# Weight tiles of a fused attention and feed-forward kernel: writes moved to ACT's queue, loads one stage earlier, whole tiles, one more resident

## The chip, the cores and the metric

The kernel runs on one core of a Trainium2 chip. The metric is the device time of one execution in microseconds (us). Engines: PE (TensorE, matrix products), DVE (VectorE), ACT (ScalarE), POOL (GpSimd), and SP (SyncE), which issues DMAs. PE's clock has two levels, 1.2 and 2.4 GHz; the profile gives the granted share of the higher one.

## What is computed

All inputs are float64 on the host; the reference in short:

```python
q_s = softmax(q, axis=-1); k_s = softmax(k, axis=2)      # [8 batches, 8 heads, 576, 64]
attn = q_s @ (k_s^T @ v)                                  # linear attention
x = attn as [4608 tokens, 512]
x = relu(x @ w_in) ** 2 @ w_out                           # 512 -> 2048 -> 512
xn = x / sqrt(mean(x * x) + 1e-6) * rms_g
out = (silu(xn @ w_gate) * (xn @ w_val)) @ w_out2         # 512 -> 1536 -> 512, float32 out
```

## The kernel before

Tokens go in nine blocks j of 512. The first feed-forward stage runs over 9 x 16 units (j, c), one for each chunk c of 128 hidden columns: `p1_A` (L526) multiplies the block by a tile of w_in into `ps_h`, applies ReLU and the square on ACT and splits the result into two float32r halves (`split`, L72: the rounded half on ACT, the rest on DVE); `p1_B` (L538), two units later, multiplies it by a tile of w_out into four accumulators. Each product is three passes over the halves (`mm3`, L92). The second stage (`p2_A`, L654, and `p2_B`, L725) does the same with gate, value and second output weights, the gate and value products by a scheme of seven half-size products (L637).

A weight tile is [128, 2, 512] float32r: 512 KB, two halves. The weights come as float64, and the core converts each tile once, in jobs that run beside the units. `tick` (L308) runs one stage of four successive jobs in this order: `d_split` of job n-3 (rounded half on ACT, L246; the rest on POOL, L247), `d_float` of n-2 (three DVE steps: L230, L238, L242), `d_words` of n-1 (POOL makes s, L211; ACT makes n, L219), `d_load` of n (the raw words by DMA from SP, L192, into one of two `raw` buffers). Behind the rounding, `d_split` writes a tile to device memory (`wd`, L253, SP) unless it is resident. The jobs of the first stage, 32 tiles, are due in the first sixteen units; those of the second stage follow over the next hundred units, where sums of converted tiles (`d_quad`, L267) are made on POOL and split and written one per unit (`d_out`, L259, with two `so` buffers, also from SP).

Eight tiles of the first stage stay resident (`NTAG`, `res1`, L126). The others pass through a ring of seven tiles `ws`; `feed` (L159) loads the next from `wd` when one is used up. In the second stage sixteen are resident (`res2`, L127).

Beside the units runs the attention of the next block for four pairs of heads (`A_STEPS`, L760): load k, q and v from SP (L334, L361), maxima, exponentials and sums on DVE and ACT, transposes and products on PE. For the first block it runs ahead of the first unit, with five ticks strewn in (the letters w in L800).

The library orders each engine's instructions ahead of time with a planner that has its own costs, starting from the order in which they are written; on the chip each queue then runs strictly in that order, and a DMA that waits holds up those behind it on the same queue. How many ticks are due by unit i:

```python
if i < FF1:                                                      # L755
    return min(NJ1 + 2, 3 + sum(d <= i for d in due.values()))
return min(NJ1 + 3 + max(0, i - FF1 - 1) * 2 // 5, len(jobs) + 3)
```

Of the kernel before, what the change touches and what calls it, by code (L numbers as in the profile page):

```python
# [8 lines left out]
F32 = mybir.dt.float32  # L9
F32R = mybir.dt.float32r  # L10
# [14 lines left out]
def attention_moe_kernel(  # L25
# [6 lines left out]
    w_out: bass.AP,  # L32
    w_gate: bass.AP,
    w_val: bass.AP,
    w_out2: bass.AP,
# [11 lines left out]
    NP = H // 2  # L47
    FF1 = w_in.shape[1] // P
    FF2 = w_gate.shape[1] // P
    SF = S // P  # L50
# [50 lines left out]
    NQ = FF2 // 2  # L101
    NTAG = 8
    NX = 8
# [79 lines left out]


    raws, words, floats = {}, {}, {}

    def halves(n, c, r):
        rows = slice(r * (DM // 2), (r + 1) * (DM // 2))
        cols = slice((2 * n + c) * P, (2 * n + c + 1) * P)
        return [w[rows, cols].rearrange("(k p) f -> p k f", p=P) for w in (w_gate, w_val)]  # L190

    def d_load(key):  # L192
        n, c = key
        r = pools["d"].tile([P, 512], U64, tag="raw", name="raw", bufs=2)
        if n == "i":
            src = w_in[:, c * P : (c + 1) * P].rearrange("(k p) f -> p k f", p=P)
            nc.sync.dma_start(out=r.rearrange("p (k f) -> p k f", k=KD), in_=src)
        elif n in ("o", "u"):
            w = w_out if n == "o" else w_out2
            nc.sync.dma_start(out=r, in_=w[c * P : (c + 1) * P, :])  # L200
        else:
            for g, src in enumerate(halves(c, int(n[0]) - 1, int(n[1]) - 1)):
                rv = r.rearrange("p (g k f) -> p g k f", g=2, k=2)
                nc.sync.dma_start(out=rv[:, g], in_=src)
        raws[key] = r
# [102 lines left out]
    def tick():  # L308
        n = ticks[0]
        for stage, ahead in ((d_split, 0), (d_float, 1), (d_words, 2), (d_load, 3)):  # L310
            if 0 <= n - 3 + ahead < len(jobs):
                key = jobs[n - 3 + ahead]
                if key is None:
                    continue
                if stage == d_split and n - 3 + ahead >= NJ1:
                    stage = d_quad
                stage(key)
        ticks[0] += 1

    def wl(key, c):  # L320
# [456 lines left out]
    with ExitStack() as ctx_a:  # L777
# [35 lines left out]
        for i, (j, c) in enumerate(units):  # L813
            if i == FF1:
                ctx_s.close()
                pools["q"] = ctx_q.enter_context(
                    tc.tile_pool(name="qp", bufs=1, reuse_waits="tile")
                )
            p1_A(j, c)
            pending.append((j, c, None))  # L820
            if len(pending) > LAG:
                p1_B(*pending.pop(0)[:2])
            while ticks[0] < n_ticks(i):
                tick()
            if i > FF1 and outs:
                outs.pop(0)()
            for n, ja, hp, f in todo.get(i, ()):
                f(ja, hp)
            if i == n1 - FF1 - 1:
                assert not outs and ticks[0] == len(jobs) + 3  # L830
# [30 lines left out]

_INS = [
    "q",
    "k",
    "v",
    "moe_w_in",
    "moe_w_out",
    "moe2_w_gate",
    "moe2_w_val",
    "moe2_w_out",  # L870
    "moe2_rms_g",
]
_OUTS = [((4608, 512), "float32")]


# [27 lines left out]
```

## Time and profile before

| | us |
|---|---|
| three runs, lowest, median, highest | 1822.58, 1823.58, 1827.39 |
| the profiled execution | 1824.28 |
| its span | 1822.5 |
| PE busy | 1750.0 (96%) |
| PE weight loads busy | 1516.4 (83%) |
| DVE busy | 1163.1 (64%) |
| ACT busy | 744.9 (41%) |
| POOL busy | 227.3 (12%) |

The span runs from the first instruction to the last; the 1.78 us around it belong to the execution. PE's busy time says where it had work, and not how fast. The shares are means over stages with different limits: the attention of the first block fills about the first 34 us, the first stage with conversions the time to some 600 us, the rest of the first stage that to 957 us, and the second stage the remainder.

### The profile page before, as it was taken

The numbers are of one execution on the slowest core, as the hardware profiler recorded it, in microseconds if no ns is written. First come the engines' busy times: TensorE is split into PE (matmuls) and PEld (weight loads), VectorE is DVE, ScalarE is ACT, GpSimd is POOL, SyncE is SP. The second block draws the span as 40 slices with busy tenths as digits, with TensorE's granted clock in tenths as the row PEclk, the third lists the DMA queues.
The fourth block names the chain that finished last, engine by engine and source line by source line (L and its number), as shares of the span: only waits on it lengthen the run. The fifth ranks groups of instructions, "written<-read, shape, count | busy, mean of one in ns | idle before, by whom it ended". The sixth has DMA issues, their size and how long they took to land.

```text
span 1822.5 us, 27487 instructions
## 1 busy us (share of the span) xinstructions
PE 1750.0 (96%) x10298; PEld 1516.4 (83%) x10298; DVE 1163.1 (64%) x2080; ACT 744.9 (41%) x1279; POOL 227.3 (12%) x265
## 2 busy tenths in 40 slices
PE   5888989999999999999999999999999999999998
PEld 3666878778877888888888989898999999999997
DVE  8987987768687654321336666675767676757544
ACT  3654545555545434333443333423233333333322
POOL 4553224333414100000000000000000000000000
PEclk9998999999999999999999999999999999999999
DMA  6778878898878855445767666767676767676673
GB/s 191 228 235 267 269 249 290 268 298 268 299 259 286 267 177 172 160 140 208 256 214 233 221 246 215 242 222 255 209 257 213 255 209 261 212 244 217 214 237 131
DMA packets 190244, 423.35 MB, mean 232 GB/s; under 512 B 57888, under 2 KB 95776, under 8 KB 188960
## 3 DMA queue, kind: packets, MB, share of 16 engines
q1 hardware_dynamic: 190112, 421.60, 69.6%
q8 instruction: 82, 1.34, 0.3%
q14 instruction: 50, 0.41, 0.1%
HBM read 361.76 MB, written 59.77 MB: 231 GB/s over the span
## 4 chain that ended last, share of the span: by engine, by line
PE 76%; DVE 10%; DMA 6%; issue 2%; ACT 2%; SPq 2%; POOL 1%; DVEq 0%; POOLq 0%; ACTq 0%
PE acc L94 31%; PE ps_h L94 15%; PE ps_x L668 8%; PE ps_y L668 8%; PE ps_v L668 8%; PE ps_w L668 4%; DMA kt<-in_k_dram 2%; DMA out_dram<-e 2%; DVE t L242 1%; DVE t L238 1%; PE ps_x L94 1%; DVE g L74 1%; DVE t L230 1%; PE ps_kv L480 1%; DVE mk L381 1%
## 5 line engine op out<-in xcount | busy, mean ns | idle before, releaser
L94 PE MATMUL ps_h<-x,ws 128*128 128x512 f32 x1296 | 328.3, 402 | 5.7 <-POOL ws L247 4.7
L94 PE MATMUL acc<-g,ws 128*128 128x512 f32 x1296 | 315.5, 392 | 7.8 <-ACT ws L246 3.4
L74 DVE TENSOR_TENSOR g<-r,g 128x512 fp32r<-128x512 f32 x252 | 186.9, 742 | 172.6 <-ACT g L73 169.9
L94 PEld LDWEIGHTS acc<-g,ws 128*128 128x128 f32 x1296 | 243.3, 188 | 62.2 <-ACT ws L246 4.2
L94 PEld LDWEIGHTS ps_h<-x,ws 128*128 128x128 f32 x1296 | 242.8, 192 | 59.2 <-POOL ws L247 7.0
L94 PE MATMUL acc<-ws,g 128*128 128x512 f32 x1080 | 267.1, 392 | 0.0
L94 PEld LDWEIGHTS acc<-ws,g 128*128 128x128 f32 x1080 | 195.5, 189 | 36.4
L73 ACT ACTIVATE g<-r 128x512 fp32r<-128x512 f32 x252 | 157.9, 627 | 35.1 <-DVE r L652 30.8
L650 ACT ACTIVATE sg<-c 128x256 f32<-128x256 f32 x108 | 56.5, 523 | 262.8 <-DVE c L683 213.3
L532 ACT ACTIVATE r<-ps_h 128x512 f32<-128x512 f32 x144 | 85.3, 593 | 190.6 <-PE ps_h L94 190.0
L683 DVE TENSOR_TENSOR u<-ps_y,p 128x512 f32<-128x512 f32 x108 | 73.9, 684 | 124.2 <-PE ps_y L668 124.2
L668 PE MATMUL ps_x<-x,ws 128*128 128x256 f32 x972 | 130.5, 284 | 10.1 <-ACT p L699 10.1
L668 PEld LDWEIGHTS ps_x<-x,ws 128*128 128x128 f32 x972 | 122.1, 191 | 11.8 <-ACT p L699 11.7
L668 PEld LDWEIGHTS ps_v<-x,ws 128*128 128x128 f32 x864 | 114.1, 191 | 6.4
L668 PE MATMUL ps_v<-x,ws 128*128 128x256 f32 x864 | 116.0, 282 | 0.0
L94 PE MATMUL ps_h<-x,w 128*128 128x512 f32 x432 | 109.2, 399 | 2.5 <-DVE x L74 1.9
L94 PE MATMUL acc<-g,w 128*128 128x512 f32 x432 | 105.7, 393 | 3.9 <-DVE g L74 1.9
L706 ACT ACTIVATE p<-ps_v 128x512 f32<-128x512 f32 x54 | 32.3, 599 | 174.8 <-PE ps_v L668 174.8
L683 DVE TENSOR_TENSOR c<-ps_v,u 128x512 f32<-128x512 f32 x54 | 37.4, 692 | 100.0 <-PE ps_v L668 99.7
L668 PE MATMUL ps_y<-x,ws 128*128 128x256 f32 x756 | 100.9, 283 | 0.0
L94 PEld LDWEIGHTS acc<-g,w 128*128 128x128 f32 x432 | 81.4, 189 | 21.9 <-DVE g L74 2.3
L94 PEld LDWEIGHTS ps_h<-x,w 128*128 128x128 f32 x432 | 80.6, 190 | 21.8 <-DVE x L74 2.5
(118 smaller groups left out, 2521.0 us busy)
## 6 DMA issues: line engine op xcount, KB each, us to landing
ws<-wd_s SPq DMA_DIRECT2D x135, 512.0 KB, 4.3
ws<-wd_a SPq DMA_DIRECT2D x117, 512.0 KB, 4.5
ws<-wd_i SPq DMA_DIRECT2D x96, 512.0 KB, 4.6
ws<-wd_o SPq DMA_DIRECT2D x96, 512.0 KB, 4.5
ws<-wd_u SPq DMA_DIRECT2D x90, 512.0 KB, 4.1
raw<-in_moe_w_out_dram SPq DMA_DIRECT2D x28, 512.0 KB, 5.3
wd_s<-so SPq DMA_DIRECT2D x24, 512.0 KB, 5.8
x2d<-e SPq DMA_DIRECT2D x36, 256.0 KB, 3.2
```

Of the source, the lines that this page charges most:

```text
L73: nc.scalar.activation(out=dst[:, 0], in_=src, func=AF.Copy)
L74: nc.vector.tensor_tensor(out=dst[:, 1], in0=src, in1=dst[:, 0].bitcast(F32), op=ALU.subtract)
L94: nc.tensor.matmul(ps, lhsT(a), rhs(b), start=first and n == 0, stop=last and n == 2)
L230: nc.vector.tensor_scalar(out=t, in0=sb, scalar1=3, scalar2=0x7FFFFFFF, op0=ALU.logical_shift_left, op1=ALU.bitwise_and,)
L238: nc.vector.scalar_tensor_tensor(out=t, in0=sb, scalar=0x80000000, in1=t, op0=ALU.bitwise_and, op1=ALU.bitwise_or)
L242: nc.vector.tensor_tensor(out=ti, in0=ti, in1=n, op=ALU.add)
L381: nc.vector.tensor_reduce(out=mk, in_=kts[j, hp].rearrange("p h c d -> p h d c"), axis=AX.X, op=ALU.max)
L532: nc.scalar.activation(out=r, in_=ps, func=AF.Relu)
L650: nc.scalar.activation(out=r, in_=h[:, :, 0], func=AF.Sigmoid)
L668: nc.tensor.matmul(ps[:, g * HF : (g + 1) * HF], w[:, wa, (2 * g + kk) * P : (2 * g + kk + 1) * P], x[:, xa, kk, :], start=first and g == ...
L683: nc.vector.tensor_tensor(out=sv(name), in0=in0, in1=in1, op=ALU.add)
L706: nc.scalar.activation(out=sv("p5"), in_=ps, func=AF.Copy)
```

## The change

- Writes of split tiles go from SP to ACT's queue and later in the program: `send` notes the tile, `flush` issues those that are old enough (two ticks for tiles of the first stage, about two units for those of the second). `keep_in_program_order` keeps such a DMA behind the ACT instructions written before it.
- Loads run one tick further ahead (four stages of lead in place of three), with three `raw` buffers in place of two. `n_ticks` gives one tick more by each unit.
- The host lays the weights out in whole tiles: a raw load is one DMA of 128 rows of 4 KB. Before, a w_in tile came in pieces of 1 KB, and a tile of gate and value weights in two DMAs.
- `NTAG` 9 in place of 8: one more resident tile in the first stage, one more in the second.
- Buffers: three `so` in place of two; the gate's `sg` moves to a pool that exists in the second stage alone; the software DMA scratch space is made smaller.

The attention is untouched. The core of the diff:

```diff
-    NTAG = 8
+    NTAG = 9
...
-        r = pools["d"].tile([P, 512], U64, tag="raw", name="raw", bufs=2)
...
+        r = pools["d"].tile([P, 512], U64, tag="raw", name="raw", bufs=3)
+        if n in ("i", "o", "u"):
+            src = {"i": w_in, "o": w_out, "u": w_out2}[n][c]
         else:
...
+            src = w_gv[int(n[1]) - 1, int(n[0]) - 1, c]
+        nc.sync.dma_start(out=r, in_=src)
...
+    late = []
+
+    def send(key, t, after):
+        late.append([after, key, t])
+
+    def flush(all=False):
+        for x in late:
+            x[0] -= 1
+        while late and (late[0][0] < 0 or all):
+            _, key, t = late.pop(0)
+            tc.keep_in_program_order(nc.scalar.dma_start(out=wd[key], in_=flat(t)))
+
     def d_split(key):
         t = slot_tile(key) if key in res1 else ring_tile()
         w_split(t, floats.pop(key), nc.gpsimd)
         if key not in res1:
-            nc.sync.dma_start(out=wd[key], in_=flat(t))
+            send(key, t, 2)
...
-            t = pools["q"].tile([P, 2, 512], F32R, tag="so", name="so", bufs=2)
+            t = pools["q"].tile([P, 2, 512], F32R, tag="so", name="so", bufs=3)
             w_split(t, f(), nc.gpsimd)
-            nc.sync.dma_start(out=wd[key], in_=flat(t))
+            send(key, t, 1)
...
-        for stage, ahead in ((d_split, 0), (d_float, 1), (d_words, 2), (d_load, 3)):
-            if 0 <= n - 3 + ahead < len(jobs):
-                key = jobs[n - 3 + ahead]
+        for stage, ahead in ((d_split, 0), (d_float, 1), (d_words, 2), (d_load, 4)):
+            if 0 <= n - 4 + ahead < len(jobs):
+                key = jobs[n - 4 + ahead]
...
         ticks[0] += 1
+        if n < NJ1 + 4:
+            flush()
...
-        r = gp.tile([P, n, HF], F32, tag="sg", name="sg", bufs=2)
+        r = pools["x"].tile([P, n, HF], F32, tag="sg", name="sg", bufs=2)
...
-            return min(NJ1 + 2, 3 + sum(d <= i for d in due.values()))
-        return min(NJ1 + 3 + max(0, i - FF1 - 1) * 2 // 5, len(jobs) + 3)
+            return min(NJ1 + 3, 4 + sum(d <= i for d in due.values()))
+        return min(NJ1 + 4 + max(0, i - FF1 - 1) * 2 // 5, len(jobs) + 4)
...
             if i > FF1 and outs:
                 outs.pop(0)()
+            if ticks[0] > NJ1 + 4:
+                flush()
...
+                flush(all=True)
...
+    nc = _bacc.Bacc(
+        "TRN2", target_bir_lowering=False, num_devices=1, dynamic_dma_scratch_size=1024
+    )
```

## Rows read from the trace of the kernel before

**Rows 1.** Windows by block: stretch, length, busy PE, PEld, DVE, ACT, POOL; clock, DMA.
```profile
33.70:169.30 135.60, 114.60 (x519) 84.90 (x518) 113.78 (x194) 73.11 (x126) 65.97 (x67) 0.94 0.73 238
169.30:273.00 103.70, 98.94 (x506) 80.81 (x505) 94.02 (x196) 51.67 (x87) 22.84 (x29) 0.98 0.82 258
273.00:372.00 99.00, 97.47 (x505) 79.47 (x504) 74.24 (x143) 50.52 (x85) 35.56 (x36) 1.00 0.86 284
372.00:471.70 99.70, 97.34 (x507) 79.00 (x506) 76.83 (x150) 53.73 (x91) 33.07 (x35) 1.00 0.88 290
471.70:577.00 105.30, 99.97 (x506) 80.88 (x505) 73.65 (x137) 50.19 (x85) 34.62 (x38) 0.98 0.80 272
577.00:676.00 99.00, 97.10 (x505) 79.59 (x504) 68.38 (x135) 48.80 (x81) 17.78 (x21) 1.00 0.73 240
676.00:773.40 97.40, 97.40 (x507) 79.95 (x506) 38.71 (x86) 40.09 (x65) 0.43 (x3) 1.00 0.50 161
```

**Rows 2.** One window of all that follows the conversions.
```profile
638.00:1822.00 1184.00, 1168.29 (x7380) 1053.95 (x7378) 660.11 (x1135) 420.31 (x732) 1.06 (x7) 1.00 0.64 216
```

**Rows 3.** Windows of the first block in two parts.
```profile
33.70:101.00 67.30, 59.32 (x286) 45.09 (x285) 65.09 (x118) 38.70 (x67) 33.87 (x33) 0.97 0.70 226
101.00:169.30 68.30, 55.28 (x235) 39.82 (x234) 48.69 (x77) 34.41 (x59) 32.10 (x34) 0.90 0.75 249
```

**Rows 4.** Groups of POOL, 101 to 169.3 us: busy, mean ns | idle before, releaser.
```profile
L247 POOL TENSOR_TENSOR ws<-t,ws 128x512 fp32r<-128x512 f32 x12 | 15.8, 1322 | 17.6 <-ACT ws L246 17.6
L211 POOL TENSOR_SCALAR s<-raw 128x512 f32<-128x512 f32 x15 | 12.5, 837 | 8.8 <-DMA raw<-in_moe_w_out_dram 5.7 <-DMA raw<-in_moe_w_in_dram 3.0
L247 POOL TENSOR_TENSOR w<-t,w 128x512 fp32r<-128x512 f32 x3 | 3.9, 1295 | 8.9 <-ACT w L246 8.9
```

**Rows 5.** Timeline, 98 to 104 us: start, duration, instruction, [idle before, releaser].
```profile
98.87 0.65 POOL L211 TENSOR_SCALAR s<-raw 128x512 f32<-128x512 f32 x1
...
99.56 0.43 DVE L230 TENSOR_SCALAR t<-s 128x512 uint32<-128x512 uint32 x1
...
100.84 0.69 DVE L242 CUSTOM_DVE_ANT_0 t<-t,n 128x1024 uint16<-128x1024 uint16 x1
...
101.63 0.63 ACT L246 ACTIVATE ws<-t 128x512 fp32r<-128x512 f32 x1 [2.39 <-DVE t L242]
...
102.34 1.28 POOL L247 TENSOR_TENSOR ws<-t,ws 128x512 fp32r<-128x512 f32 x1 [2.82 <-ACT ws L246]
...
103.59 0.65 POOL L211 TENSOR_SCALAR s<-raw 128x512 f32<-128x512 f32 x1
```

**Rows 6.** Waits of SP, 0 to 600 us: total us, times, longest.
```profile
SPq L253 <- POOL ws L247: 68.7, 21, 5.6
...
SPq L350 <- DVE qn L455: 40.3, 9, 7.8
SPq L263 <- POOL so L247: 37.4, 16, 6.0
```

**Rows 7.** DMA issues on the page: count, KB each, median us to landing.
```profile
raw<-in_moe_w_out_dram SPq DMA_DIRECT2D x28, 512.0 KB, 5.3
...
raw<-in_moe_w_in_dram SPq DMA_DIRECT2D x16, 512.0 KB, 4.6
```

**Rows 8.** Groups of DVE, 101 to 169.3 us.
```profile
L242 DVE CUSTOM_DVE_ANT_0 t<-t,n 128x1024 uint16<-128x1024 uint16 x15 | 12.0, 802 | 1.2
L238 DVE SCALAR_TENSOR_TENSOR t<-s,t 128x512 uint32<-128x512 uint32 x14 | 11.6, 827 | 0.3
```

**Rows 9.** Groups of DVE, 33.7 to 101 us.
```profile
L238 DVE SCALAR_TENSOR_TENSOR t<-s,t 128x512 uint32<-128x512 uint32 x15 | 15.8, 1051 | 0.1
L242 DVE CUSTOM_DVE_ANT_0 t<-t,n 128x1024 uint16<-128x1024 uint16 x16 | 15.4, 965 | 0.2
```

**Rows 10.** A group of DVE, 0 to 700 us: the attention's maxima.
```profile
L381 DVE TENSOR_REDUCE mk<-kt 128x128 f32<-128x640 f32 x31 | 40.4, 1303 | 35.7 <-DMA kt<-in_k_dram 29.2 <-POOL kvd L793 4.7 <-POOL kt L338 1.5
```

**Rows 11.** Line 253: issues of a write from SP, ns min/median/max.
```profile
L253 SPq DMA_DIRECT2D wd_i<-ws x12: 320/334/506, 38.9 to 162.7; - x12
```

More of the change, by code (lines that the diff above doesn't have):

```diff
@@ L32, in attention_moe_kernel @@
     w_out: bass.AP,
-    w_gate: bass.AP,
-    w_val: bass.AP,
+    w_gv: bass.AP,
     w_out2: bass.AP,
@@ L47, in attention_moe_kernel @@
     NP = H // 2
-    FF1 = w_in.shape[1] // P
-    FF2 = w_gate.shape[1] // P
+    FF1 = w_in.shape[0]
+    FF2 = w_out2.shape[0]
     SF = S // P
@@ L309, in tick @@
         n = ticks[0]
-        for stage, ahead in ((d_split, 0), (d_float, 1), (d_words, 2), (d_load, 3)):
-            if 0 <= n - 3 + ahead < len(jobs):
-                key = jobs[n - 3 + ahead]
+        for stage, ahead in ((d_split, 0), (d_float, 1), (d_words, 2), (d_load, 4)):
+            if 0 <= n - 4 + ahead < len(jobs):
+                key = jobs[n - 4 + ahead]
                 if key is None:
                     continue
-                if stage == d_split and n - 3 + ahead >= NJ1:
+                if stage == d_split and n - 4 + ahead >= NJ1:
                     stage = d_quad
@@ L829, in attention_moe_kernel @@
             if i == n1 - FF1 - 1:
-                assert not outs and ticks[0] == len(jobs) + 3
+                assert not outs and ticks[0] == len(jobs) + 4
+                flush(all=True)
                 ctx_q.close()
@@ L859, in attention_moe_kernel @@
             p2_B(*u)
[L862 to L873, printed above, removed]
 def kernel(**inputs):
@@ L881 @@
     from concourse.bass_utils import run_bass_kernel_spmd as _run
-    nc = _bacc.Bacc("TRN2", target_bir_lowering=False, num_devices=1)
-    arrays, args = {}, []
-    for name in _INS:
-        a = _np.ascontiguousarray(inputs[name])
-        if a.dtype == _np.float64:
-            a = a.view(_np.uint64)
-        arrays[f"in_{name}_dram"] = a
-        args.append(
-            nc.dram_tensor(
-                f"in_{name}_dram", a.shape, _mybir.dt.from_np(a.dtype), kind="ExternalInput"
-            ).ap()
-        )
@@ L895, with tiles @@
-    for i, (shape, dtype) in enumerate(_OUTS):
-        dt = _mybir.dt.from_np(_np.dtype(dtype))
-        args.append(nc.dram_tensor(f"out_{i}_dram", shape, dt, kind="ExternalOutput").ap())
+    P = 128
+    def tiles(name, dims, order, shape):
+        t = _np.ascontiguousarray(inputs[name]).view(_np.uint64).reshape(dims).transpose(order)
+        return _np.ascontiguousarray(t).reshape(shape)
+    a = {name: _np.ascontiguousarray(inputs[name]) for name in ("q", "k", "v")}
+    d, ff = inputs["moe_w_in"].shape
@@ new lines @@
+    a["w_in"] = tiles("moe_w_in", (d // P, P, ff // P, P), (2, 1, 0, 3), (ff // P, P, d))
+    a["w_out"] = tiles("moe_w_out", (ff // P, P, d), (0, 1, 2), (ff // P, P, d))
+    d, ff = inputs["moe2_w_gate"].shape
+    dims = (2, d // P // 2, P, ff // P // 2, 2, P)
+    t = [
+        tiles(name, dims, (0, 4, 3, 2, 1, 5), (2, 2, ff // P // 2, P, d // 2))
+        for name in ("moe2_w_gate", "moe2_w_val")
+    ]
+    a["w_gv"] = _np.concatenate(t, axis=-1)
+    a["w_out2"] = tiles("moe2_w_out", (ff // P, P, d), (0, 1, 2), (ff // P, P, d))
@@ new lines @@
+    a["rms_g"] = inputs["moe2_rms_g"]
+    nc = _bacc.Bacc(
+        "TRN2", target_bir_lowering=False, num_devices=1, dynamic_dma_scratch_size=1024
+    )
+    arrays, args = {}, []
+    for name in a:
+        arrays[f"in_{name}"] = _np.ascontiguousarray(a[name])
+        dt = _mybir.dt.from_np(arrays[f"in_{name}"].dtype)
+        shape = arrays[f"in_{name}"].shape
+        args.append(nc.dram_tensor(f"in_{name}", shape, dt, kind="ExternalInput").ap())
+    b, h, s, e = a["q"].shape
+    out = nc.dram_tensor("out", (b * s, h * e), _mybir.dt.float32, kind="ExternalOutput")
@@ L898 @@
     with _tile.TileContext(nc) as tc:
-        attention_moe_kernel(tc, *args)
-    r = _run(nc, [arrays], core_ids=[0])
-    got = tuple(r.results[0][f"out_{i}_dram"] for i in range(len(_OUTS)))
-    return got[0]
+        attention_moe_kernel(tc, *args, out.ap())
+    return _run(nc, [arrays], core_ids=[0]).results[0]["out"]
```

13 lines of the change are left out of this document (removed).

## The prediction

> **What bounds the kernel now.** I read the page first: TensorE (PE) is busy 96% of the span (it stands in the table of the page), so a change can gain only what PE loses in some stage. Then the windows, cut at every sixteenth unit of the first feed-forward stage (a unit is one chunk c of one block j; I call a row of sixteen units a block). The seventh window [rows 1] is a block with nothing in its way: 97.4 us, PE busy throughout at full clock. The six before it do the same matmuls beside weight conversion and attention, and take 135.6, 103.7, 99.0, 99.7, 105.3 and 99.0 us: 38.2, 6.3, 1.6, 2.3, 7.9 and 1.6 us more, 57.9 us together. Behind 638 us PE is busy 1168.3 of 1184.0 us [rows 2] and POOL does nothing: no conversion runs there. So the change can act on those 57.9 us, and mostly on the first block.
>
> The first block, cut in two [rows 3], has two limits. Up to 101 us VectorE (DVE) is busy 65.09 of 67.30 us, 97%: it is the bound there. From 101 to 169.3 us DVE is down to 48.69 of 68.30 us, POOL to 32.10, ACT to 34.41, PE to 55.28 at a clock of 0.90: no engine is full, so the stretch is held by a chain. The POOL rows [rows 4] say of what kind: fifteen tiles are split (12 in ring buffers and 3 residents), and before the splits POOL stood idle 17.6 + 8.9 us for ACT's half of the split, and before the first conversion step 8.8 us for the raw DMA. The timeline [rows 5] shows one round: POOL makes s at 98.87, DVE starts on it at 99.56 and ends L242 at 101.53, ACT rounds at 101.63, POOL subtracts at 102.34, and only then, at 103.59, POOL makes the next s. That is 4.7 us for a tile, and 68.3 us by fifteen tiles is 4.55: the stages written to overlap run one tile after another. PE wants two tiles a unit, that is one in 97.4/32 = 3.04 us.
>
> **The change part by part**, against the profiled execution, 1824.28 us (1822.5 of span and 1.78 around it; the median is 0.70 lower).
>
> *Loads one tick further ahead, three raw buffers, writes off SP.* Before, the load of job n stands on SP behind the write of job n-3, which waits for POOL's subtraction. SP waited 68.7 us in 21 such writes, 3.3 us each, and 37.4 us in 16 writes of the second kind [rows 6]. After it, SP holds no write of a weight tile; a load waits for the raw buffer alone, freed two stages before it, and its data has two ticks to come instead of one. The median raw load lands 4.6 us (w_in) or 5.3 us (w_out) after its issue [rows 7], which is more than one tick of 4.55 and less than two. So the raw wait goes, and POOL can make the s of a later tile before it subtracts an earlier one: the loop of [rows 5] opens. What is late next is DVE. Its work in the second stretch is 48.69 us; packed as densely as in the first stretch its instructions get longer, because there POOL runs beside it more: L238 from 827 to 1051 ns and L242 from 802 to 965 ns [rows 8, 9]. That is 14 x 0.224 + 15 x 0.163 = 5.6 us, so 54.3 us, and at 97% filling 56.0 us. 68.3 - 56.0 = 12.3: I take 12 us gained. The bounds: nothing, if the loop stays; and 68.3 less PE's own need, 15 tiles x 3.04 = 45.6, which is 22.7 us. I take the DVE end since the stretch just before it is held by DVE.
>
> In the first stretch DVE is full, so I take zero. One tick more ahead of the first unit moves one tile's three DVE steps behind the attention of block 0; that can cost at most their 0.43 + 0.69 + 0.69 = 1.8 us (durations with POOL idle [rows 5]; L238 taken as L242), and DVE's whole idle time there is 2.2 us, so the bounds are +1.8 and -2.2.
>
> *The same in blocks 2 to 6*, 19.7 us over. kmax of the attention (L381) kept DVE waiting 29.2 us for the k tiles in the first 700 us [rows 10], and those loads stand on SP in order behind the writes. SP's waits there: 37.4 us for the split tiles, which goes, and 40.3 us for the previous q tile (L350 on DVE's qn) [rows 6], which stays as the attention stays. So about half of SP's blocking goes, but a wait on SP only counts where attention ends last, and the attention buffers hold the next loads back anyway. I take a third of 19.7, 6 us, with 0 and 19.7 as bounds. The single loads for the gate and value tiles (24 DMAs fewer to issue, 0.33 us each on SP [rows 11]) lie within this term.
>
> *What is added: 77 writes on ACT's queue* (23 in the first block, 54 of the second stage). No DMA was issued from ACT, so its price is open: the nearest row is SP's, 334 ns for the median write [rows 11], and for 77 of them 25.7 us of ACT over about 570 us. The cover is ACT's idle time, 33.9 of 68.3 us in the second stretch [rows 3]. Behind a write stand ACT's roundings, exponentials and ReLUs. A write leaves two ticks after its split, some 9 us later, where POOL's subtraction takes 1.3 us, so I count no wait with it. Bounds: zero, and all 25.7 us if the cover is gone; I take zero, because ACT idled before the split in waiting for DVE. Three split buffers in place of two carry the later writes.
>
> *Whole tiles in memory.* w_out was read in whole 4 KB rows before and landed in 5.3 us; w_in was read in 1 KB pieces and landed in 4.6 us [rows 7]. Short pieces don't show as slower, so zero; between the two, 0.7 us on 16 loads, 11 us either way if they all stood in the loop, and they leave it by the extra tick.
>
> *One more resident, the gate's buffer moved.* One ring tile less in the first block, 8 loads less in the later blocks and 9 in the second stage, at places where PE waits for no weight; 15.7 us of idle time in 1184 [rows 2] is the whole that could be touched, by less than 2 us either way. Zero.
>
> The sum: 0 - 12 - 6 + 0 = -18, so 1824.28 - 18 = 1806.
>
> **The rivals.**
> *PE becomes the bound* of the second stretch, and the attention loads run freely: -22.7 there and two thirds of 19.7, -13, give 1788.6. For it: DVE had 19.6 us idle in that stretch. Against: DVE is full just before.
> *The loop stays.* The order on each engine's queue is fixed ahead by a planner with its own idea of times. If it still puts the subtraction before the next s, only part of the 8.8 us of raw waits goes, say 3 us, and the 6 us of the later blocks: 1815. For it: the code of before also meant to overlap. Against: its loads came too late for that.
> *POOL takes it back from DVE.* When the loop opens, POOL's 30 steps run while DVE works. If each holds a DVE step back for half its length, that is 15 x 0.66 + 15 x 0.42 = 16.2 us; already paid are 15 x 0.11 for L242 (802 against 690 ns with POOL idle [rows 5, 8]) and 14 x 0.14 for L238, 3.6. So 48.7 + 12.6 = 61.3, at 97% 63.2: 5 us gained in place of 12, and with the 6 us 1813. The Trainium skill (SBUF — State Buffer, "Terms") says that DVE and GpSimd share a pair of ports under a lock held for the full instruction, and that the loser blocks; the trace agrees as far as L242 goes from 690 to 965 ns where POOL is busier.
> *Slower: ACT is held by the writes.* ACT runs in order, and a write that is not ready stops the roundings and ReLUs behind it. On SP a write waited 3.3 us. It decides from 18/77 = 0.23 us a write on PE's path. At 0.4 us each, 31 us: 1824.3 - 18 + 31 = 1837. For it: the DMA's price on ACT is unknown. Against: the two ticks of delay and ACT's idle half.
>
> **How the numbers follow.** Forecast 0.48 (1800 to 1813), PE bound 0.13, loop stays 0.17, POOL takes it back 0.13, slower 0.09. A measurement here tells 0.3% (5.5 us) from no change, so faster means under 1818. Faster: 0.46 of the forecast, 0.13, 0.11 of 0.17, 0.11 of 0.13: 0.81. Same: the rest of these, 0.02 + 0.06 + 0.02, and 0.01 of the last: 0.11. Slower: 0.08. The range goes down to the PE-bound case, 1789, and up past the two small gains to 1822, with their second term at nothing.
>
> **What would show it.** After: a first block of about 123 us; in its second half two s steps of POOL or more between the end of DVE's L242 and the subtraction of that tile, DVE over 90% busy, and POOL's idle time before the splits under 15 us (26.5 before); no wait of SP for POOL; kmax waiting for k under 20 us; DMA rows of ACT of about 0.33 us with no wait for POOL; the stretch of the second stage as long as before within 2 us. A first block over 130 us, or ACT waiting at its writes, makes the forecast wrong; gains behind 700 us would mean that I missed a cause.

## The result, and the profile after

The changed kernel takes 1837.01 us at the median of four runs (1835.74 to 1839.59), the kernel before 1825.19 beside it (1822.58 to 1827.39): a ratio of 1.0067, 95% interval 1.0048 to 1.0086. It is slower by 12 us where 18 us less were forecast. The profiled execution took 1837.18 us, 1835.4 of them span.

Windows of the kernel after at the same units as [rows 1] (stretch, length, busy PE, PEld, DVE, ACT, POOL, clock, DMA share, GB/s):

```profile
33.80:169.20 135.40, 110.56 (x520) 80.27 (x519) 120.62 (x210) 69.35 (x125) 73.60 (x69) 0.96 0.75 253
169.20:277.60 108.40, 99.88 (x505) 81.20 (x504) 89.71 (x189) 54.18 (x91) 30.28 (x34) 0.97 0.76 238
277.60:385.60 108.00, 100.38 (x506) 81.55 (x505) 68.19 (x137) 48.30 (x81) 24.85 (x27) 0.97 0.70 227
385.60:488.60 103.00, 98.74 (x505) 80.48 (x504) 64.88 (x137) 47.45 (x81) 24.59 (x27) 0.98 0.72 237
488.60:593.80 105.20, 100.17 (x505) 81.65 (x504) 67.90 (x137) 48.34 (x81) 24.96 (x27) 0.97 0.73 233
593.80:695.30 101.50, 99.10 (x506) 81.00 (x505) 66.79 (x137) 49.05 (x82) 27.33 (x28) 0.98 0.71 229
695.30:792.60 97.30, 97.30 (x506) 79.89 (x505) 44.50 (x92) 45.70 (x76) 15.52 (x15) 1.00 0.65 217
```

Against [rows 1], the first block is as long as before (135.4), the five behind it take 526.1 us in place of 506.8, the seventh is the same. The rest is the tail, from the start of the last first-stage unit to the end: 868.8 us in place of 875.1. So +19.3 in units 16 to 95, -6.3 in the tail, nothing in units 0 to 15. POOL shows another difference: it still splits in the seventh block (15.52 us busy, 0.43 before), so the conversion is spread over more units.

What PE and ACT wait for from 165 to 700 us (us in total, times, longest), in the kernel before:

```profile
PE ps_x L94 <- DVE kvd L493: 7.8, 5, 4.7
...
ACT so L246 <- DMA wd_s<-so: 21.4, 15, 3.6
...
ACT so L246 <- DMA wd_a<-so: 14.5, 12, 4.0
...
ACT so L246 <- DMA wd_u<-so: 13.8, 8, 2.6
```

and in the kernel after:

```profile
PE ps_x L93 <- DVE kvd L497: 22.7, 7, 6.3
...
ACT so L236 <- DMA wd_s<-so: 33.6, 15, 5.4
...
ACT so L236 <- DMA wd_a<-so: 24.7, 11, 4.5
...
ACT so L236 <- DMA wd_u<-so: 11.5, 5, 4.5
...
ACT r L536 <- POOL so L237: 7.1, 2, 4.2
```

PE waits longer for `kvd`, the k-v matrix that the last product of the next block's attention needs (two lines of the kernel make it, 25.0 us in place of 11.5 with both), and ACT's roundings of the second-stage tiles wait for a free `so` buffer, 69.8 us in place of 49.7. The last line is a ReLU that stood behind a write which waited for POOL's split. The longest wait of PE, 6.27 us at 226.00, shows how the two belong together. ACT in the timeline (start, duration, instruction, [idle before, releaser]):

```profile
209.04 0.33 ACTq L249 DMA_DIRECT2D wd_a<-so  x1
209.42 0.60 ACT L536 ACTIVATE r<-ps_h 128x512 f32<-128x512 f32 x1 [4.17 <-POOL so L237]
...
215.33 0.63 ACT L236 ACTIVATE so<-s 128x512 fp32r<-128x512 f32 x1 [3.99 <-DMA wd_a<-so]
215.39 0.36 ACTq L249 DMA_DIRECT2D wd_s<-so  x1
...
216.42 0.58 ACT L72 ACTIVATE qT<-ps_q 128x512 fp32r<-128x512 f32 x1
...
220.54 0.63 ACT L236 ACTIVATE so<-s 128x512 fp32r<-128x512 f32 x1 [1.72 <-DMA wd_s<-so]
...
221.64 0.72 ACT L435 ACTIVATE ke<-kt 128x640 f32<-128x640 f32 x1
...
292.73 0.33 ACTq L249 DMA_DIRECT2D wd_a<-so  x1
...
296.86 0.63 ACT L236 ACTIVATE so<-t 128x512 fp32r<-128x512 f32 x1 [1.67 <-DMA wd_a<-so]
```

and DVE:

```profile
217.03 0.69 DVE L73 TENSOR_TENSOR qT<-ps_q,qT 128x512 fp32r<-128x512 f32 x1 [3.27 <-ACT qT L72]
...
224.58 0.27 DVE L497 TENSOR_SCALAR kvd<-ps_kv,rk 64x64 fp32r<-64x64 f32 x1
```

A write goes out at 209.04; the rounding behind it waits 3.99 us for its landing; behind that stand the query's rounding (216.42) and, behind the next such wait, the exponential of k (221.64). DVE idles 3.27 us, makes `kvd` from 224.58 on, and PE goes on at 226.00. In the six waits of PE for `kvd` over 1.5 us, ACT had stood at a landing or at POOL's split in the 18 us before. The last two ACT rows show why buffers were short: behind the write at 215.39 the next one goes out at 292.73, so the three tiles rounded last, up to 220.54, kept all three `so` buffers for some 70 us, and the next rounding (296.86) waited for that write's landing. This recurs: on the mean of the 54 writes the issue comes 27.3 us after the end of POOL's split.

### The profile page after: what moved, and what is told of

The parts are those of the page before. It is cut to its first block, busy times and chain, and to the rows that moved or that the text cites. A ratio compares the mean times of both kernels' runs of the same rounds, so it can differ in the third digit from the quotient of the medians.

```text
span 1835.4 us, 27344 instructions
## 1 busy us (share of the span) xinstructions
PE 1754.6 (96%) x10298; PEld 1518.2 (83%) x10298; DVE 1144.0 (62%) x2080; ACT 740.2 (40%) x1279; POOL 239.3 (13%) x265
## 4 chain that ended last, share of the span: by engine, by line
PE 81%; DVE 5%; DMA 3%; ACT 1%; issue 1%; POOL 0%; SPq 0%; DVEq 0%; POOLq 0%; ACTq 0%
PE acc L93 33%; PE ps_h L93 17%; PE ps_x L672 8%; PE ps_v L672 8%; PE ps_y L672 8%; PE ps_w L672 4%; PE ps_x L93 1%; DVE t L228 1%; DMA wd_a<-so 1%; PE ps_kv L484 1%; DVE t L232 1%; DMA wd_s<-so 1%; PE ps_q L471 1%; DVE t L220 1%; DVE g L73 0%
## 5 line engine op out<-in xcount | busy, mean ns | idle before, releaser
L73 DVE TENSOR_TENSOR g<-r,g 128x512 fp32r<-128x512 f32 x252 | 181.5, 721 | 207.2 <-ACT g L72 204.5
L93 PE MATMUL ps_h<-x,ws 128*128 128x512 f32 x1188 | 304.1, 405 | 5.1 <-POOL ws L237 4.9
L93 PEld LDWEIGHTS ps_h<-x,ws 128*128 128x128 f32 x1188 | 225.5, 194 | 55.2 <-POOL ws L237 7.5
L93 PE MATMUL acc<-ws,g 128*128 128x512 f32 x972 | 243.2, 393 | 2.3 <-ACT g L72 2.3
L93 PEld LDWEIGHTS acc<-ws,g 128*128 128x128 f32 x972 | 175.2, 189 | 35.9 <-ACT g L72 3.7
L93 PE MATMUL ps_h<-x,w 128*128 128x512 f32 x540 | 135.0, 397 | 1.4 <-POOL w L237 1.2
L93 PEld LDWEIGHTS ps_h<-x,w 128*128 128x128 f32 x540 | 99.8, 189 | 23.1 <-POOL w L237 1.6
L93 PEld LDWEIGHTS acc<-g,w 128*128 128x128 f32 x432 | 80.8, 188 | 19.3 <-DVE g L73 2.6
```

The lines of the kernel that those rows point to most:

```text
L73: nc.vector.tensor_tensor(out=dst[:, 1], in0=src, in1=dst[:, 0].bitcast(F32), op=ALU.subtract)
L93: nc.tensor.matmul(ps, lhsT(a), rhs(b), start=first and n == 0, stop=last and n == 2)
```

## Experiments

Times are medians beside runs of the kernel before on the same chip; the lengths of stretches come from one profiled execution each. The changed kernel issues 23 first-stage and 54 second-stage writes; expectations below count 13 and 64, which is wrong, and nothing hangs on it. Versions of the kernel before that need more buffers also have the smaller DMA scratch space. Most runs vary one part of the change, in the kernel after or alone in the kernel before. Where "writes" are named, the second-stage ones alone are varied; the run without the pin and the one with all writes from SP take in the first-stage ones.

**The pin alone**, in the kernel after:

```diff
-            tc.keep_in_program_order(nc.scalar.dma_start(out=wd[key], in_=flat(t)))
+            nc.scalar.dma_start(out=wd[key], in_=flat(t))
```

> The changed kernel with the second-stage and first-stage writes still issued late through ACT's queue, but no longer pinned to the program order: the planner may put each write where it likes among ACT's instructions. Theory P (pin): the planner runs the second-stage roundings some 100 us ahead of program order while a pinned write stays behind a gate rounding traced before it, so that two of the three so buffers are held and each rounding on ACT waits for the landing of the write before it. Unpinned writes come right behind their splits; ACT's waits at L236 for wd writes (53 us in 0 to 600 now) fall to under 20, the single PE waits of 1.8 to 6.3 us for kvd in units 16 to 95 go, unit 143 starts at 947 to 953 us instead of 966.6, and the time is 1816 to 1823. Rival Q (ACT's queue itself): a DMA write that waits for its POOL split stands in ACT's queue whatever its place, and holds the roundings behind it; the writes come earlier and so wait longer: time 1833 or more. Rival L (the load lead and the third raw buffer set the planner's order): no change, 1835 to 1839.

Measured: 1846.08 us, ratio 1.0125 (1.0106 to 1.0143). My first theory fell: ACT's waits for landings are all but gone (6.5 us from 165 to 700), and it is slower still. Q's time came, but not by its mechanism alone: units 16 to 47 take 241.3 us (202.8 before) with DVE 88% busy, and units 64 to 95 take 193.4 us, no longer than two blocks with nothing in their way (97.3 each). The conversion has run ahead.

**The writes from SP at the split**, as before, the rest as changed:

```diff
-            send(key, t, 1)
+            nc.sync.dma_start(out=wd[key], in_=flat(t))
```

> The changed kernel with its second-stage writes alone put back where they were: issued by SP right at the split, not late and not on ACT; the 13 or so first-stage writes stay late on ACT, and the raw buffers, the layout and the resident tiles stay as changed. Theory P (pinned late writes on ACT cost the 19 us of units 16 to 95): unit 143 starts within 3 us of the kernel before's 947.4, the tail keeps its gain of 6, time 1815 to 1821. Rival Q (any write on ACT's queue): the same, 1815 to 1821, so this run tells P and Q only from L. Rival L (lead and third raw buffer): still 1833 or more.

Measured: 1808.65 us, ratio 0.9923 (0.9901 to 0.9944); units 16 to 95 take 494.2 us and PE's waits for `kvd` are 4.4 us in all (25.0 in the kernel after). So the writes, late and on ACT, cost the changed kernel 1.4% of the time, more than its whole loss.

**Late writes on ACT, pinned, with three buffers, alone in the kernel before:** `send` and `flush` of the diff for `d_out` only.

> The kernel before with one part of the change alone: second-stage split tiles written late through ACT's queue, pinned, with three buffers (a smaller DMA scratch makes room); raw buffers, layout, load lead, first-stage writes and residents as before. Theory P: this alone brings the loss of units 16 to 95, 14 to 20 us, with single PE waits of 2 to 6 us for kvd; unit 143 starts at 961 to 968 us and the time is 1839 to 1846, the tail as before. Rival L: no loss without the deeper load lead, 1822 to 1829. Between them (1830 to 1838) both are needed for the whole.

Measured: 1841.07 us, ratio 1.0097 (1.0080 to 1.0114); units 16 to 95 take 520.9 us. The part alone brings the loss, without the deeper loads.

**Late and pinned, but on SP** (the same place in the program, the other queue):

```diff
+    def write(key, t, eng):
+        tc.keep_in_program_order(eng.dma_start(out=wd[key], in_=flat(t)))
...
-            tc.keep_in_program_order(nc.scalar.dma_start(out=wd[key], in_=flat(t)))
+            write(key, t, nc.scalar if ticks[0] <= NJ1 + 4 else nc.sync)
```

> The changed kernel with its second-stage writes still late and pinned to the program order, one flush after the split, but in SP's queue instead of ACT's. With the writes at the split and from SP the time was 1808.7, late and from ACT 1837.0; this run and the next part the two. Theory H (hold: it is the late place that keeps so buffers full for long, so that roundings on ACT wait whatever queue writes them): PE waits for kvd in 165 to 700 stay at 20 us or more (25.0 now, 4.4 with SP at the split), time 1828 to 1840. Theory A (it is ACT's queue: a write that waits for its POOL split, and the landing behind it, stands in front of the attention's rounding): waits of ACT for POOL's split at L536 and L537 go, PE waits for kvd 4 to 10 us, time 1806 to 1816.

Measured: 1823.74 us, ratio 0.9996 (0.9987 to 1.0006), between the two theories.

**On ACT, but at the split:**

```diff
-            send(key, t, 1)
+            tc.keep_in_program_order(nc.scalar.dma_start(out=wd[key], in_=flat(t)))
```

> The changed kernel with its second-stage writes on ACT's queue, pinned right behind their own rounding instead of late, so that ACT stands still until POOL's split of 1.5 to 1.6 us is done, 64 times in units 16 to 95. Theory H (late place): buffers come free early, and the 64 standstills cost some ACT time but ACT is half idle there: PE waits for kvd 4 to 12 us, time 1808 to 1822. Theory A (ACT's queue): ACT waits some 64 times 2 us for POOL in front of attention steps, PE waits for kvd 20 us or more, time 1830 to 1850.

Measured: 1851.99 us, ratio 1.0158 (1.0141 to 1.0175): the slowest of all, so H alone is wrong. The four corners, as ratios to the kernel before:

| second-stage writes | from SP | from ACT, pinned |
|---|---|---|
| at the split | 0.9923 | 1.0158 |
| late | 0.9996 | 1.0067 |

ACT's queue costs 0.7% late and 2.4% at the split. Lateness costs 0.7% on SP, and on ACT it gives 0.9% back. Each corner also has the planner's order that goes with it, so these are prices of queue and place with their orders. Two things act, and the rows show both. First, ACT from 165 to 700 us with its writes at the split (the four largest waits for POOL's split):

```profile
ACT r L536 <- POOL so L237: 15.4, 7, 6.1
ACT g L72 <- POOL so L237: 12.4, 5, 3.6
...
ACT r L537 <- POOL so L237: 4.5, 5, 1.8
...
ACT x L72 <- POOL so L237: 1.8, 1, 1.8
```

A write in ACT's queue that is not ready holds ReLUs and roundings that have nothing to do with it; these rows and one of 1.5 us for the query come to 35.6 us here, to 8.6 in the kernel after, and there is none of them with SP's writes. Second, the pace of the conversions: POOL's splits into `so` by 100 us (stretch, length, POOL busy and count, clock, DMA share, GB/s), with writes on ACT at the split:

```profile
170.00:270.00 100.00, 18.45 (x13) 0.95 0.82 272
270.00:370.00 100.00, 30.29 (x21) 0.93 0.92 324
370.00:470.00 100.00, 27.68 (x21) 0.93 0.86 297
```

on SP at the split:

```profile
170.00:270.00 100.00, 10.42 (x7) 0.98 0.77 245
270.00:370.00 100.00, 21.20 (x15) 1.00 0.87 294
370.00:470.00 100.00, 17.78 (x13) 1.00 0.89 293
470.00:570.00 100.00, 27.08 (x19) 1.00 0.89 294
```

and in the kernel after:

```profile
270.00:370.00 100.00, 11.87 (x9) 0.97 0.70 231
370.00:470.00 100.00, 11.66 (x9) 0.98 0.71 234
470.00:570.00 100.00, 13.05 (x9) 0.97 0.76 243
...
670.00:770.00 100.00, 11.85 (x9) 1.00 0.64 209
```

From ACT at the split the conversions crowd into 300 us, 13, 21 and 21 by 100 us, at a clock of 0.93 to 0.95; from SP at the split they go 7 to 19; late writes keep buffers full and hold them at 9 on ACT and 8 to 10 on SP, and on ACT each hold stands in front of the attention. How long a tile stays in its buffer goes with this: on the mean of the 54 writes, the issue comes 0.6 us after the end of POOL's split from ACT at the split, 12.0 from SP at the split, 27.3 late on ACT and 26.7 late on SP. So SP's queue holds the buffers a while too, which is the likely brake on running ahead; that it is what makes SP's writes the cheaper ones was not tried.

**A fourth `so` buffer** in the kernel after (`bufs=4`):

> The changed kernel with four so buffers instead of three, the late writes on ACT pinned as they are. By the run without the pin (1846, ACT's waits for landings down from 75 us to 5, and the whole second-stage conversion crowded into units 16 to 50) two things are to be told apart. Theory P2 (a pinned write keeps two of three buffers, the rest alternate on landings of 4 to 5 us, and ACT stands in line behind each): a fourth buffer leaves two free, ACT's waits at L236 for wd writes fall from 75 us to 30 to 50, units 16 to 95 cost 505 to 512 us instead of 526, time 1817 to 1825. Rival C (crowding: whatever lets the conversions run ahead puts them in front of the attention steps on DVE; the landings were a brake): less braking, units 16 to 47 longer than the 216 us of now (220 to 240), time 1836 to 1848.

Measured: 1831.59 us, ratio 1.0041 (1.0027 to 1.0055), units 16 to 95 at 522.4 us, ACT's waits for landings hardly less (66.8 from 165 to 700). A buffer more gives back some 5 us, hardly clear of noise (the intervals touch); neither theory's size holds.

**Resident tiles.** Eight tags in the kernel after (`NTAG = 8`):

> The changed kernel with eight resident tags, as before, instead of nine; the gate buffers stay in their new pool. Theory R (one more resident shifts the choice of residents, so that at the end of a second-stage block no weight load is issued just ahead of the output writes): the tail (last first-stage unit to the end) goes back from 868.8 to 874 to 876 us, the output writes land again in about 5 us instead of 3.4 at the median, and the time is 1842 to 1845. Rival G (the moved gate buffers, or the smaller scratch): the tail stays at 868 to 870 and the time at 1836 to 1839.

Nine tags alone in the kernel before:

> The kernel before with one more resident tile alone (nine tags; a smaller DMA scratch makes room). Theory R: the tail loses 6 us as in the changed kernel (875.1 to 868 to 870), the first-stage units stay within 2 us; time 1815 to 1821. With eight tags in the changed kernel the tail was 874.9 again, but the time rose by 3.5 only, since its units 16 to 95 came out 2 us shorter, so this run is to show whether the resident also costs something ahead. Rival: the gain of the tail needs the moved gate buffers too: tail 874 to 876, time 1822 to 1827.

Eight tags with the writes from SP:

> The changed kernel with second-stage writes from SP (1808.7), with eight resident tiles instead of nine. The tail goes back to 873 to 876 us. Theory X (one more resident costs units 16 to 95 some 10 us or more wherever SP writes): units 16 to 95 fall from 494 to 485 to 488 us, near PE's own 484, time 1804 to 1809. Rival Y (the resident by itself costs nothing; in the kernel before it met the two raw buffers and split loads): units 16 to 95 stay within 4 us of 494, time 1812 to 1818.

Measured: 1840.48 us, ratio 1.0088 (1.0068 to 1.0109); 1829.60, ratio 1.0029 (1.0016 to 1.0041); 1814.21, ratio 0.9955 (0.9937 to 0.9973). The tail is 874.9, 869.1 and 874.8 us: it goes with the resident, and none of the parts tried alone below moves it out of 872.8 to 875.1. PE's waits from 960 us on with eight tags, in the kernel before

```profile
PE ps_x L668 <- ACT p L699: 10.1, 8, 2.0
```

and with nine, in the kernel after:

```profile
PE acc L93 <- ACT g L72: 4.3, 4, 2.0
```

Eight waits go, of 0.5 to 2.0 us. Before each, ACT's squares for the norm of the next block had waited 2.6 to 4.1 us for the landing of the writes of a finished block, and the copy `p` that PE needs stood behind them. In the kernel before a weight load is issued at 1058.67, just ahead of such writes (1060.00); the output writes land 5.2 us after their issue at the median there, 3.4 with nine tags. That this load makes them late was read and not tried by itself. In units 16 to 95 the resident made no difference with SP's writes (493.5 against 494.2 us), but 16 us alone in the kernel before (523.2 against 506.8). For that I have no cause.

**Parts alone in the kernel before:** three raw buffers with the longer lead; a third `so` buffer, written from SP at the split; the whole tiles in memory; the moved gate buffers.

> The kernel before with the third raw buffer and the load lead of four alone (a smaller DMA scratch makes room); layout, writes and residents as before. Theory D (DVE sets the first block's pace; opening POOL's loop frees nothing): units 0 to 15 take 134 to 138 us as in all kernels so far, ACT's wait for raw loads after unit 16 falls, time 1820 to 1826. The forecast's step (the loop costs the second half of the first block 12 us): units 0 to 15 at 121 to 126 us and the time at 1809 to 1815.

> The kernel before with a third so buffer alone, its writes issued by SP at the split as before (a smaller DMA scratch makes room). In the changed kernel with these writes on SP, units 64 to 95 took 194.0 us against 204.4 before, and the time was 1808.7. Theory B (the third buffer does it: the rounding on ACT waits less for landings, so conversions are done by unit 88 instead of 95): units 64 to 95 at 193 to 198, ACT's waits for wd landings from 50 us down to 30 to 40, time 1812 to 1818. Rival W (whole-tile loads, the third raw buffer and the deeper load lead do it, by ending ACT's and POOL's waits for raw, 28.7 and 18.0 us of ACT before): units 64 to 95 at 202 to 206, time 1821 to 1826.

> The kernel before with the weights laid out in whole tiles alone. By the forecast: nothing, 1821 to 1827. Theory B2 (it takes part in the gain of 12 us ahead of the tail that the changed kernel with SP's writes has, and that neither the third raw buffer nor the third so buffer brought alone: one load a tile of 4 KB a partition in place of two of 128 rows' pieces of 1 KB lands sooner, so ACT's waits for raw, 41.9 us in 165 to 700, fall below 25): units 16 to 95 at 494 to 500, time 1811 to 1818.

> The kernel before with the second stage's gate buffers moved into the pool that opens behind the first stage, alone; nothing of it runs before unit 143. By its mechanism: units 0 to 95 unchanged to 1 us, tail unchanged, 1821 to 1827. Theory O (any edit gives the planner another order, and the order moves units 16 to 95 by up to 10 us): units 16 to 95 off by more than 3 us one way or the other with the same queues and the same work.

Measured: 1823.09 us, ratio 0.9993 (0.9979 to 1.0007); 1823.53, ratio 1.0003 (0.9986 to 1.0020); 1819.91, ratio 0.9988 (0.9975 to 1.0002); 1822.34, ratio 1.0003 (0.9991 to 1.0016). None can be told from no change. Units 16 to 95 take 509.6, 505.8, 500.3 and 505.8 us (506.8 before), so the gate buffers, which do no work there, leave them within 1 us. The layout's 6.5 us less stand in the fastest of its ten runs (1817.27); its interval allows 4.6 us at most for the whole kernel. Where the 12.6 us come from that the changed kernel with SP's writes wins in these units stays open. The raw buffers with the longer lead alone also test a part of the forecast's largest term, with the writes still on SP: units 0 to 15 take 131.9 us, 3.7 less than before, where the whole was to give 12; but the ninth resident alone, which does not touch the load lead, gave 132.0.

**All writes from SP at the split**, the first-stage ones too (`send(key, t, 2)` likewise replaced):

> The changed kernel with all writes back on SP at the split, the 13 first-stage ones too; left of the change are raw buffers, load lead, layout, resident and the third so buffer. Theory D (DVE sets the first block): units 0 to 15 at 131 to 137 us as in every kernel so far, no matter which queue writes; time 1804 to 1814, as with the first-stage writes on ACT (1808.7). Rival F (SP holds the first block when writes that wait for POOL stand in front of its raw loads, as in the kernel before): POOL and ACT wait for raw again, units 0 to 15 at 138 us or more, time 1812 to 1820.

Measured: 1810.80 us, ratio 0.9930 (0.9916 to 0.9945), units 0 to 15 at 135.0 us. SP again waits 74.1 us for POOL in the first-stage writes (68.7 in [rows 6]), and the first block is no longer. The 23 first-stage writes cost or give nothing on either queue that can be told.

**The first block.** The scaling that makes s on ACT, with the writes from SP (`nc.scalar.activation(out=s, ..., func=AF.Copy, scale=2.0**-112)` in place of the POOL instruction):

> The changed kernel with second-stage writes from SP (1808.7), and the scaling that makes s moved from POOL (0.92 us each in units 0 to 15) to ACT, to tell what sets the first block. Theory D2 (POOL's work slows DVE: L232 takes 1.0 us in the first block against 0.8 where POOL is less busy, and DVE is 89% busy): POOL falls from 74 to about 47 us busy there, DVE's instructions get shorter, units 0 to 15 fall to 125 to 131 us, time 1800 to 1806. Theory D1 (DVE's own work at its lone speed sets the pace): DVE's means stay within 4%, units 0 to 15 at 133 to 137, time 1806 to 1813. Rival K (ACT becomes late, with about 0.65 us more per tile in front of its roundings): units 0 to 15 at 138 or more, time over 1813.

The writes from SP, and DVE's addition left out:

```diff
-        nc.vector.tensor_tensor(out=ti, in0=ti, in1=n, op=ALU.add)
```

> The changed kernel with second-stage writes from SP (1808.7), and DVE's last instruction of each converted tile, the addition of the low bits (L232, 1.0 us each, 29 us in units 0 to 15), left out: the low bits of the weights are missing from what it computes. Theory D1 (DVE's own work sets the first block; 89% busy there): units 0 to 15 fall by 15 to 25 us, to 111 to 121 us, then near PE's own 97 us; time 1780 to 1795. Rival S (each tile is a chain through POOL, DVE, ACT and POOL whose length over two s buffers sets 4.2 us a tile): only the microsecond of L232 leaves the chain, and half of that the pace, units 0 to 15 at 126 to 132, time 1798 to 1806. Rival Z (POOL's splits of 1.5 us behind ACT's roundings, or loads, set it): 133 to 137, time 1805 to 1811.

Measured: 1805.45 us, ratio 0.9902 (0.9887 to 0.9917), units 0 to 15 at 133.9; and 1788.85, ratio 0.9813 (0.9791 to 0.9834), units 0 to 15 at 124.9. The first block with SP's writes, with s on ACT, and without the addition:

```profile
34.20:170.40 136.20, 109.14 (x521) 79.12 (x518) 120.64 (x210) 69.37 (x125) 73.59 (x69) 0.99 0.75 252
```

```profile
34.00:167.90 133.90, 111.96 (x520) 83.37 (x519) 122.56 (x217) 85.33 (x154) 41.75 (x39) 0.94 0.76 253
```

```profile
30.90:155.80 124.90, 112.70 (x540) 83.43 (x539) 94.15 (x184) 70.63 (x126) 64.71 (x71) 0.96 0.84 279
```

With s on ACT, POOL loses 32 us of work and the block 2; without the addition, DVE loses 26 and the block 11. The first of the two is no clean test of D2, as DVE's conversion steps did not get shorter together: 64.0 us in place of 65.6, one from 995 to 828 ns a piece, the other two from 726 up to 773 and from 479 up to 561. The second shortens DVE's work and the chain of each tile at once, and its 124.9 us lie between D1 and S, with DVE 75% busy. So DVE's work, or the chain through it, weighs more than POOL's here, and what else holds the block stays open.

**On top of s on ACT**: the queries' subtraction on POOL for all blocks (`nc.gpsimd` in place of `nc.vector`), and three buffers each for `s` and `n`.

> The changed kernel with second-stage writes from SP and s made on ACT (1805.5), and the subtraction of the queries' maximum moved from DVE to POOL for all eight row blocks (0.84 to 1.05 us each on DVE, 6 in units 0 to 15). Theory D1: DVE loses 5 to 6 us in units 0 to 15 and about 0.9 us in front of each query tile later; units 0 to 15 at 128 to 132, units 16 to 95 up to 4 us less, time 1796 to 1803. Rival W (POOL waits behind its splits and takes longer for the subtraction, so the query chain is late): units 16 to 95 longer by 2 to 8 us, time 1806 to 1814.

> The changed kernel with second-stage writes from SP and s made on ACT (1805.5), with three buffers each for s and n instead of two. Theory S (the release of s is the rest of the chain in units 0 to 15): these units fall from 133.9 to 124 to 130 us, time 1795 to 1803. Theory D1 (DVE, 92% busy there, is the bound and a buffer gives it no time): 132 to 136 us, time 1802 to 1809. Rival C (conversions run further ahead and crowd the attention steps): units 16 to 47 longer than the 203 us of now by 5 or more, time over 1810.

Measured: 1812.42 us, ratio 0.9941 (0.9921 to 0.9962), units 0 to 15 at 137.8 and 16 to 95 at 501.9: the time and the longer units are W's. And 1803.57 us, ratio 0.9897 (0.9877 to 0.9917), units 0 to 15 at 130.9: the fastest version that does all the work, and faster than both kernels. Against two buffers, its interval does not tell it from 0.9902.

## Why the prediction was wrong

| us of the profiled span | forecast | after | writes from SP |
|---|---|---|---|
| ahead of unit 0 | 0 | +0.1 | +0.6 |
| units 0 to 15 | -12 | -0.2 | +0.5 |
| units 16 to 95 | -6 | +19.3 | -12.6 |
| units 96 to 142 | 0 | 0 | 0 |
| tail | 0 | -6.3 | -6.4 |
| the whole span | -18 | +12.9 | -17.9 |

*The writes on ACT, taken at zero, failed.* The step was argued from two sentences: "A write leaves two ticks after its split, some 9 us later, where POOL's subtraction takes 1.3 us, so I count no wait with it", and "Three split buffers in place of two carry the later writes". Both held for the order in the program. On the chip the planner's order counts, which runs the second-stage roundings ahead and leaves the pinned writes behind (tiles rounded by 220.54, written from 292.73 on, above). So ACT did wait for POOL, 8.6 us, and the buffers were not free: its waits for landings went from 49.7 to 69.8 us and stood in front of the attention. Measured by the four corners the term is 1.0067 - 0.9923, 1.4% or 26 us: half for the late place and half for ACT's queue when they are added in this order; in the other order the queue costs 2.4% and the late place gives 0.9% back. That lies at the upper bound, 25.7, but not for the reason of the bound. The writes' own issues cost nothing that shows:

```profile
L249 ACTq DMA_DIRECT2D wd_s<-so x24: 326/327/358, 215.4 to 807.7; - x24
```

It is 327 ns at the median, as on SP [rows 11], and lies beside the instruction ahead of it (215.39 in the timeline above, under the rounding from 215.33 to 215.96). The slower rival named the place, ACT's roundings behind a write that is not ready, and its time, 1837, was the one that came. That agreement is in part luck: its price, 0.4 us a write in the whole, was a guess that left out the buffers, and it kept the 18 us of gains, which did not come. The Trainium skill (DMA: Bandwidth & Descriptors, "Issuing engines are not separate DMA queues") says that issuing from several engines saves only the sequencer's issue time. The 327 ns agree with an issue that is short beside its landing (4.4 us at the median), but the sentence names the gain alone: moving the second-stage writes to ACT cost 0.7 to 2.4% here.

*The first block, minus 12, failed by its premise.* The loop of [rows 5] did open, as the sum had it. The second half of the block in the kernel after, POOL's groups (answering to [rows 4]) and the windows of both halves ([rows 3]):

```profile
L237 POOL TENSOR_TENSOR ws<-t,ws 128x512 fp32r<-128x512 f32 x12 | 19.2, 1605 | 0.0
L201 POOL TENSOR_SCALAR s<-raw 128x512 f32<-128x512 f32 x16 | 15.0, 938 | 29.5 <-DVE t L228 18.7 <-issue 9.0 <-ACT g L72 1.8
L237 POOL TENSOR_TENSOR w<-t,w 128x512 fp32r<-128x512 f32 x3 | 5.1, 1714 | 0.0
```

```profile
33.80:101.00 67.20, 55.97 (x269) 40.47 (x268) 60.17 (x107) 35.62 (x64) 34.02 (x35) 0.97 0.70 225
101.00:169.20 68.20, 54.59 (x253) 39.80 (x252) 60.45 (x104) 33.73 (x61) 39.58 (x35) 0.95 0.80 281
```

POOL's idle time before the splits fell from 26.5 us to nothing, and it waits for DVE instead. But DVE is busy 60.45 of 68.20 us there where 48.69 had been counted. The conversion is not what grew: its three steps on DVE took 12.0, 11.6 and 9.1 us there before (the first two in [rows 8]), 32.7 together, and take 33.0 after:

```profile
L232 DVE CUSTOM_DVE_ANT_0 t<-t,n 128x1024 uint16<-128x1024 uint16 x15 | 16.0, 1063 | 0.8
L228 DVE SCALAR_TENSOR_TENSOR t<-s,t 128x512 uint32<-128x512 uint32 x15 | 10.3, 689 | 0.3
L220 DVE TENSOR_SCALAR t<-s 128x512 uint32<-128x512 uint32 x16 | 6.7, 418 | 4.9 <-POOL ws L237 4.0 <-POOL w L237 0.8
```

The last step went from 802 to 1063 ns, more than the 965 that I took, and the middle one from 827 to 689, where I took 1051. What grew is the other work: over the whole block DVE has 120.62 us in place of 113.78 and 16 instructions more, though the three steps take 65.5 in place of 70.6. Steps of the attention that stood behind the block are run in it now; six maxima of k (7.8 us), for one, where there were three (4.0). So the 48.69 us were a stretch's share under the old order, not an amount to be packed.

"POOL takes it back from DVE" was the nearer rival for this block by its number, but its mechanism, longer steps, is not what filled the stretch. Overlap does lengthen a step: with SP's writes the last one took 0.68 us in the three cases of the block with no POOL instruction beside it, and 1.00 in the 21 with one all along. The Trainium skill (SBUF — State Buffer, "Terms") has DVE and GpSimd lock each other out of a shared port pair; these two figures agree in direction. What that overlap costs the block is open, since less work on POOL hardly made the three steps shorter together (64.0 against 65.6 us, above).

*The later blocks, minus 6*, failed too. kmax does wait less for k in the kernel after, 14.0 us against 29.2 in [rows 10], as SP's queue is freer:

```profile
L385 DVE TENSOR_REDUCE mk<-kt 128x128 f32<-128x640 f32 x31 | 40.0, 1291 | 18.8 <-DMA kt<-in_k 14.0 <-POOL kvd L797 4.7
```

Units 16 to 95 were longer all the same, as ACT was what came last. With the second-stage writes back on SP the wait is nearly the old one,

```profile
L385 DVE TENSOR_REDUCE mk<-kt 128x128 f32<-128x640 f32 x32 | 41.4, 1294 | 32.5 <-DMA kt<-in_k 27.3 <-POOL kvd L797 4.7 <-issue 0.4
```

and these units are 12.6 us shorter. So the wait for k did not set their time in either, and that 12.6 lies within the bounds of 0 to 19.7 is luck.

*Layout* and the *gate's buffer* at zero stand, by the times. *One more resident* at zero was wrong: the 15.7 us of PE's idle time behind 638 us [rows 2] were called out of reach, and 10 of them were the eight waits at the ends of the blocks, which the waits of that stretch show.

That the version with SP's writes came out 17.9 us shorter in span, where 18 were forecast, is a coincidence: no term of the sum has its size.

## What to carry to other kernels

Before a DMA is moved to a compute engine's queue, read what stands behind it there, and ask in which order the engine really runs: a delay written in the program is none if the instructions it should let pass have been moved ahead and the buffer it holds is what they need. When a buffer is released also goes with how far work runs ahead: here the shortest and the longest stay in the buffer were both slower than the middle one, so try queue and place apart. An engine's busy time in a stretch forecasts that stretch only if the same work stays in it, so ask which work of a later stretch can be pulled in.

## What the runs showed of the hardware that I had not expected

- The quicker landings are in the slower kernel: 4.4 us at the median for the second-stage writes in the kernel after, 6.1 with these writes from SP at the split. What stood behind the writes counted for more here than how long they took.
- Short waits go with more than their length. From 165 to 700 us PE waits 28.5 us in the kernel after and 7.6 with SP's writes, 20.9 less, but units 16 to 95 differ by 31.9. The other 11 us are PE's own busy time for the same products, 498.3 against 487.2 us; the granted clock over the stretch is 0.97 in the one and 1.00 in the other.
- What a DVE step loses to POOL beside it moves from step to step: with s on ACT the last step of a conversion fell from 995 to 828 ns and the two before it rose, so 32 us less work on POOL left the three together nearly as they were (64.0 for 65.6 us in the first block).
